# Linear attention into a gated long convolution on one core: another hand-written order of issue, and idle products at 14 places instead of 11

## The chip, the cores and the metric

The kernel runs on one core of a Trainium2 chip. Times are device microseconds, from the profile's clock or from timed runs of the whole program; the median of three timed runs is 264.11 us (264.1 to 265.25). Five engines work side by side, each through its own queue in order: TensorE (PE; its weight loads are PEld), VectorE (DVE), ScalarE (ACT), GpSimd (POOL) and SyncE (SP). In this kernel GpSimd and SyncE issue DMAs, and ScalarE issues one.

## What is computed

Two stages. The first is attention with random features, for 8 batches of 8 heads, 576 rows and 64 columns, with 128 features:

```python
h = proj - sq;  h = h - np.max(h, axis=-1, keepdims=True)
phi = np.exp(h) / np.sqrt(m)                   # proj = x @ omega.T, x = q or k, scaled
kv = einsum('bhsm,bhsd->bhmd', k_p, v);  z = sum(k_p, axis=2)
out = einsum('bhsm,bhmd->bhsd', q_p, kv) / (einsum('bhsm,bhm->bhs', q_p, z) + 1e-6)
```

The second takes that output as x (8 batches, 576 rows, 512 columns):

```python
x1, x2, x3 = split(x @ w_proj)
x2_conv = irfft(rfft(x2, axis=1) * rfft(filter, axis=0), n=576, axis=1)
y = (x1 * x2_conv * x3) @ w_out
```

## The kernel before, in words

**Tiling.** Each batch's 576 rows are four tiles of 128 and 64 rows left over; the left rows of two batches make one tile more ("left keys", "left queries", "left out"). Keys and queries are turned with TensorE (`transposes`) and copied to SBUF by VectorE or ScalarE. `key_features` and the query products go into PSUM, and ScalarE takes the exponential. `max_to_c` and `scale_values` weigh the values on VectorE (the factor that replaces the maximum). "Sums" is 40 products of 65 columns per batch, which ScalarE copies to `kv`. "Turn out" is eight products for each tile, `normalise` on VectorE, and a turn back (`turn_runs`, `turn_back`) into `xt`.

**Second stage.** "Gates" are the x1 and x3 products of `xt` with the weights, multiplied on VectorE. The transform over 576 points is products with small tables: 576 is 3 times 192, and the bins are kept in classes of even and odd ones. "Fold" and "rest" build the folded rows, "forward" transforms, SyncE moves halves of the spectrum to the other partitions (`sp`, `xw`), VectorE multiplies by the filter's spectrum, "inverse" transforms back, and "out" multiplies by w_out and stores.

**The filter.** `load_filter` loads the filter in two parts (288 KB each in SBUF), `fold_filter` folds them on VectorE, SyncE moves the pieces to `fd` and `fl`, `filter_transform` makes five groups of products, and `split_out` evicts each on ScalarE (two evictions) and sends it by SyncE to `hps` and `hqs`.

**What sets the order.** The program is not issued as it is written. The class `Plan` records every instruction (L182), numbers it (1,466 operations; products into one tile of one stage count as one), and `order` (L215) returns them in the order of the constant `ORDER` (L26), after it has made sure that data come before use. `issue` (L234) then issues them in that order; all recorded instructions carry line 250. Every engine's queue is therefore that list with the others' entries left out. Tiles that share a name share a few buffers, and these are handed out in the order of issue: the order also decides which batch's values share a buffer, and what a load has to wait for.

**Idle products.** `FILL` (L92) names operations on TensorE in front of which `issue` puts products of ones with ones (L239) into the bank that the operation is about to write; nobody reads them.

**Names used below.** Operations 1 and 6 load the two halves of batch 0's keys; 86 and 87 load the filter; 655 to 664 fold it on VectorE and 665 to 674 move the pieces on SyncE; 689, 682, 704, 697 and 675 are the filter's products. 110 scales batch 0's values, 119 is batch 0's sums, 120 their copy. 200 and 202 turn back batch 1's normalised rows. 220 loads batch 3's values, 349 the left values of batches 4 and 5.

Of the kernel before, what the change touches and what calls it, by code (L numbers as in the profile page):

```python
# [23 lines left out]
CROSSED = {"keys": 8, "queries": 8, "out": 8}  # L24

ORDER = """  # L26
25 34 39 32 38 40 35 37 33 36 31 28 29 30 4 42 49 41 43 50 51 6 0 1 3 56 55 21 139 5 22 44 68 45 24
10 75 137 46 62 23 64 63 9 2 54 52 53 57 65 83 60 59 58 76 61 81 7 66 82 78 89 141 90 14 613 48 69
209 91 101 103 85 70 47 84 142 92 80 93 138 102 612 94 95 96 72 74 67 11 77 157 79 71 611 73 112 114
158 104 615 160 116 151 12 105 106 107 152 145 162 118 627 159 115 161 154 117 221 153 156 155 111 8  # L30
20 16 87 108 109 97 99 110 119 19 210 113 98 120 167 614 168 163 164 127 128 121 122 183 165 184 129
130 123 131 18 132 15 124 125 126 148 86 174 176 185 166 186 133 177 227 630 169 170 222 140 187 134
178 180 179 100 228 171 172 233 135 229 136 173 175 231 616 655 657 628 629 147 146 149 619 17 658
716 647 656 234 649 181 672 235 182 673 212 247 211 236 248 194 621 625 660 144 195 674 639 668 188
196 189 620 190 245 641 246 191 640 197 192 193 626 198 199 319 320 224 648 226 642 623 722 650 202
215 13 203 281 204 200 201 205 206 143 689 691 690 675 676 659 696 622 663 724 679 255 695 219 150
618 617 792 692 223 216 214 213 624 661 677 237 238 634 225 794 694 257 731 662 793 207 788 643 715
208 645 795 239 230 259 261 664 666 681 717 293 240 720 671 725 669 294 287 288 232 732 790 651 295
249 723 719 670 297 693 321 665 323 322 737 290 292 218 733 789 250 241 251 635 721 252 734 738 296
298 260 217 678 283 667 791 253 243 254 644 680 357 262 256 258 780 646 242 289 358 711 718 282 263  # L40
299 782 291 697 264 268 269 712 276 351 345 220 277 270 278 631 636 300 653 698 301 682 302 713 699
714 265 266 273 267 274 684 363 704 309 706 244 364 311 705 683 781 735 736 726 275 303 729 783 304
305 306 702 366 359 688 739 707 652 700 368 686 361 740 637 638 313 365 785 784 315 367 420 360 362
654 307 308 346 369 747 314 728 370 727 786 385 386 787 317 316 751 318 748 271 272 310 340 755 341
342 429 312 430 752 753 749 750 756 327 335 387 388 754 328 730 336 279 757 381 329 796 337 280 764
893 348 284 382 687 371 758 332 423 285 372 632 333 334 417 957 959 685 798 710 797 424 389 343 344
373 892 765 324 432 325 799 383 969 894 899 374 709 326 708 421 492 766 896 352 703 745 434 384 741
396 746 971 398 88 286 760 759 898 762 338 339 742 961 958 633 425 884 701 761 431 427 970 960 743
963 354 433 744 330 331 962 763 972 375 897 376 392 964 395 901 355 803 903 377 907 908 895 817 885
390 482 888 349 353 394 379 347 819 902 378 889 769 814 805 770 985 815 800 987 802 801 816 977 916  # L50
917 979 804 806 905 807 808 818 820 821 809 399 823 886 906 397 810 822 499 455 400 887 456 426 391
914 824 393 915 825 500 826 900 773 774 428 978 912 811 812 771 412 772 767 913 768 909 413 414 439
776 775 980 827 501 910 986 493 409 481 911 494 440 904 410 503 856 857 865 866 932 858 933 930 931
988 411 495 497 415 862 416 863 419 356 928 973 975 929 778 777 779 974 976 441 842 844 401 402 403
350 845 843 847 864 867 934 487 831 833 935 937 404 846 828 830 829 442 418 405 849 851 406 965 967
813 435 437 832 848 496 502 936 918 834 850 436 443 852 836 483 438 919 890 835 859 853 891 504 966
944 860 945 938 837 855 968 838 924 925 553 498 554 922 839 939 940 923 407 408 449 450 981 452 451
1150 920 1152 446 380 457 840 1010 491 490 448 861 854 868 927 458 921 1012 983 444 453 454 869 559
1077 521 522 1085 517 1151 560 1153 996 459 445 505 1092 476 506 477 447 998 518 871 872 997 1000
1086 555 989 982 999 478 984 557 479 480 463 464 471 946 991 870 472 948 473 950 951 947 1087 873  # L60
465 926 942 460 461 523 877 841 878 1011 1013 1014 1088 1089 1090 507 519 1163 1162 524 520 941 488
1091 1078 949 1164 1158 1165 462 508 990 1107 952 468 879 992 466 469 470 1108 467 943 509 1093 510
1109 489 474 1160 525 953 475 1105 511 880 1007 1106 422 881 882 1009 1008 1079 1110 874 562 561 955
954 883 1080 993 1123 1159 564 994 1081 512 1124 995 532 875 1016 486 1101 956 1102 1094 1001 1002
1015 1161 534 1166 1024 1168 1096 1017 1003 526 1026 1154 1156 1038 513 1004 1098 1040 1127 1021 563
1022 1128 1006 1018 1005 1023 1155 1103 1104 531 556 558 533 1025 1125 484 485 1167 515 1019 1028
1157 1027 528 1126 530 1039 1121 1030 1082 1029 1031 1169 1032 1020 569 1122 876 535 527 536 529 585
586 1100 1170 1035 1036 1172 548 537 1095 1041 549 1083 1042 1115 1130 1129 1037 1044 538 550 539
565 1084 540 566 1116 567 568 1171 541 545 1043 542 1045 1034 1046 570 546 514 547 1099 543 544 1058
587 589 1117 1059 1118 1052 1053 1120 1054 1047 1097 551 552 1033 1119 1111 1112 588 1113 1114 1174  # L70
1064 580 575 1131 516 1347 1176 1065 577 1067 1132 1173 582 1133 1068 1203 571 1135 572 573 579 581
1205 1048 576 1349 578 1270 1271 574 1066 1069 1049 1175 1348 1177 1134 1350 583 1136 1143 1204 1206
1050 1051 1285 1278 1355 1139 584 1144 590 1190 1207 1140 1357 1137 606 1138 1189 1191 1061 591 592
607 1062 608 1063 1193 1279 1186 1182 601 602 1188 609 1187 593 603 1183 610 1280 1192 598 1141 1200
1184 594 1142 1351 1356 1282 1185 1201 1202 1209 1284 595 1302 1303 1353 599 600 1283 1208 1358 1281
1055 1352 1354 596 1145 1060 1146 1148 1056 597 1147 1300 604 605 1298 1299 1301 1057 1210 1149 1294
1073 1343 1195 1295 1287 1286 1074 1345 1076 1194 1075 1196 1197 1211 1213 1272 1217 1219 1273 1318
1231 1319 1316 1317 1233 1296 1297 1320 1214 1274 1275 1321 1232 1218 1215 1216 1199 1198 1070 1071
1212 1220 1235 1234 1221 1288 1072 1276 1277 1178 1228 1314 1180 1229 1315 1323 1322 1289 1222 1223
1224 1225 1230 1248 1344 1237 1236 1346 1310 1311 1249 1245 1179 1246 1247 1250 1312 1290 1292 1293  # L80
1363 1304 1181 26 1291 1365 1305 1313 1306 1359 1238 1361 1307 1308 1239 1241 1330 1309 1227 1266
1267 1324 1332 1325 1328 1326 1269 1268 1331 1333 1364 1382 1384 1327 1329 1366 1240 1383 1334 1385
1379 1335 1380 1386 1226 1387 1388 1251 1360 1252 1253 1381 1396 1398 1336 1397 1362 1389 1393 1260
1337 1395 1400 1399 1394 1242 1254 1261 1402 1390 1339 1401 1391 1403 1404 1405 1338 1341 1340 1342
1375 1367 1255 1243 1244 1369 1438 1439 1377 1262 1256 1441 1442 1435 1436 1443 1440 1437 1376 1410
1378 1392 1424 1411 1412 1407 1425 1426 1406 1408 1413 1414 1409 1428 1415 1371 1373 1421 1368 1263
1422 1423 1416 1427 1417 1372 1264 1429 1430 1418 1431 1265 1444 1445 1257 1370 1420 1432 1374 1434
1447 1446 1258 1259 1433 1419 1457 1451 1448 1458 1452 1463 1464 1449 1454 1450 27 1455 1460 1461
1462 1459 1453 1465 1456
"""  # L90

FILL = {  # L92
    22: (25,), 69: (3,), 72: (7,), 75: (17,), 78: (61,), 89: (4,), 91: (8,), 101: (4,), 103:
    (6,), 127: (6,), 157: (4,)
}

SIZE = {FP32: 4, UINT16: 2, BF16: 2, FP16: 2, mybir.dt.uint32: 4}


class Region:  # L100


    __slots__ = ("lo", "hi", "mask")

    def __init__(self, ap):
# [1296 lines left out]
```

## Time and profile before

| what | value |
|---|---|
| timed runs (median, range) | 264.11 us, 264.1 to 265.25 |
| the profiled execution, whole | 264.05 us |
| its span, first to last instruction | 262.3 us |
| mean granted TensorE clock | 0.993 |
| TensorE busy, products | 248.5 us, 95%, 2554 products (145 of them idle products) |
| VectorE, ScalarE, GpSimd busy | 230.8 us (88%), 212.9 us (81%), 59.6 us (23%) |
| last product ends, last store issued | 258.4 us, 259.0 us |

The page's second part cuts the span into 40 slices of 6.6 us; each digit is a busy share in tenths. The table of stretches gives, for a stretch in us: its length, then the busy time and the number of instructions of TensorE's products, its weight loads, VectorE, ScalarE and GpSimd, then the granted TensorE clock, the busy share of the DMA engines and the GB/s moved. A timeline row gives start, length, engine, line, operation, "out<-in", shapes and count; brackets hold the engine's idle time before it and what released it. In the chain that ended last, each row is start, length, and the work that held the end up at that time. Products are pipelined: a row's length holds the latency of its last product, so the next row can start before this one ends.

### The profile page before, as it was taken

What the parts mean: (1) busy time and instruction counts of PE and PEld (TensorE: products, weight loads), DVE (VectorE), ACT (ScalarE), POOL (GpSimd) and SP (SyncE); (2) the same over time, 40 slices, a digit from 0 to 9 for tenths busy, and PEclk for the clock granted to TensorE, in tenths of its full rate; (3) what the DMA queues carried; (4) which work ended last, traced back from release to release, by engine and by line L of the source; (5) the groups of instructions that cost most, each with busy time, mean ns of one, the idle gap of its engine ahead of it and who ended that gap; (6) DMA issues with size and microseconds to landing.
All of it is one profiled execution on the core that took longest, in us unless ns stands there. A gap on an engine that the chain in (4) does not pass through costs nothing.

```text
span 262.3 us, 6466 instructions
## 1 busy us (share of the span) xinstructions
PE 248.5 (95%) x2554; PEld 151.4 (58%) x2554; DVE 230.8 (88%) x549; ACT 212.9 (81%) x334; POOL 59.6 (23%) x80
## 2 busy tenths in 40 slices
PE   7977789999999999999999999999999999999994
PEld 6955656445547745645646655556457655456641
DVE  7899899998898997899989797999996889889980
ACT  5897498999999999869898779998996578567653
POOL 8393674440720093500314000000000000000000
PEclk9998899999999999999999999999999999999999
DMA  6999999999998599993692905103121421524626
GB/s 85 164 157 192 193 184 209 193 182 199 125 152 141 137 121 160 150 126 112 132 119 16 186 18 133 53 2 84 60 80 42 139 89 55 170 49 125 240 94 228
DMA packets 68854, 33.42 MB, mean 127 GB/s; under 512 B 39707, under 2 KB 63192, under 8 KB 68824
## 3 DMA queue, kind: packets, MB, share of 16 engines
q0 software_dynamic: 59088, 16.85, 63.2%
q1 hardware_dynamic: 9592, 15.96, 20.6%
q8 instruction: 20, 0.33, 0.5%
q10 hardware_dynamic: 144, 0.20, 0.2%
q14 instruction: 10, 0.08, 0.1%
HBM read 33.72 MB, written 9.44 MB: 165 GB/s over the span
## 4 chain that ended last, share of the span: by engine, by line
PE 60%; DMA 18%; DVE 10%; ACT 4%; POOL 3%; issue 2%; SPq 2%; DVEq 0%; POOLq 0%; ACTq 0%
PE h L250 48%; PE a L250 10%; DMA vl<-in_v_dram 4%; DMA vn<-in_v_dram 3%; DMA sp<-sp 3%; DVE sp L250 3%; DMA hps<-osb 3%; DMA sp<-x 2%; DMA kn<-in_k_dram 2%; PE a L239 2%; SPq L250 2%; DMA xw<-xr 1%; ACT osb L250 1%; DVE vc L250 1%; DVE xb L250 1%
## 5 line engine op out<-in xcount | busy, mean ns | idle before, releaser
L250 PE MATMUL h<-xt,wproj 128*128 128x512 bf16 x256 | 64.3, 379 | 0.1
L250 ACT CAST x<-h 128x512 bf16<-128x512 f32 x68 | 39.9, 600 | 9.0 <-PE h L250 8.3
L250 PEld LDWEIGHTS <-wproj 128*128 128x128 bf16 x384 | 30.8, 98 | 25.9 <-issue 2.4
L250 POOL DMA_DIRECT2D qn<-in_q_dram x26 | 23.2, 898 | 57.8 <-PE h L250 46.1
L250 ACT ACTIVATE eqt<-a 128x1024 bf16<-128x1024 f32 x32 | 33.0, 1048 | 3.0 <-PE a L250 2.8
L250 ACT ACTIVATE osb<-h 128x512 f32<-128x512 f32 (+4 forms) x53 | 29.6, 570 | 6.8 <-PE h L250 5.2
L250 ACT ACTIVATE ek<-a 128x1024 bf16<-128x1024 f32 x32 | 33.0, 1050 | 1.1 <-PE a L250 1.0
L250 PE MATMUL h<-wproj,xf 128*128 128x512 bf16 x128 | 32.1, 379 | 0.4 <-DVE kt L250 0.4
L250 PE MATMUL h<-wout,yt 128*128 128x512 bf16 (+2 forms) x132 | 31.4, 373 | 0.0
L250 DVE TENSOR_TENSOR x<-h,x 128x512 bf16<-128x512 f32 x32 | 21.9, 684 | 3.5 <-PE h L250 2.6
L250 DVE TENSOR_TENSOR xb<-a,rden 128x512 bf16<-128x512 f32 x36 | 24.2, 682 | 0.7
L250 ACT CAST sp<-h 128x512 bf16<-128x512 f32 x32 | 18.5, 596 | 4.8 <-PE h L250 4.8
L250 PEld LDWEIGHTS <-yt 128*128 128x128 bf16 x132 | 12.2, 98 | 13.0 <-DVE yt L250 0.4
L250 PEld LDWEIGHTS <-xf 128*128 128x128 bf16 x128 | 11.7, 98 | 13.1 <-issue 1.3
L250 PEld LDWEIGHTS <-sp 128*128 128x128 bf16 x160 | 13.7, 98 | 6.9 <-issue 1.0
L250 ACT COPY xt<-h 128x1024 bf16<-128x1024 bf16 x16 | 16.3, 1025 | 0.4 <-PE h L250 0.2
L250 PE MATMUL h<-x,fwb 128*128 128x512 bf16 x56 | 15.5, 379 | 0.0
L250 PE MATMUL a<-qt,om 64*128 64x512 bf16 x64 | 11.8, 383 | 2.0 <-ACT eqt L250 0.9
L250 PE MATMUL a<-om,kt 64*128 64x128 bf16 x256 | 11.8, 218 | 1.8 <-ACT ek L250 1.0
L250 ACT COPY qt<-h 128x1024 bf16<-128x1024 bf16 x12 | 12.1, 1016 | 1.7 <-PE h L250 1.7
L250 PEld LDWEIGHTS <-eqt 128*128 128x128 bf16 x256 | 11.1, 99 | 3.6 <-issue 0.7
L250 PE MATMUL a<-kv,eqt 128*128 128x65 bf16 x256 | 12.6, 195 | 0.4 <-DVE xb L250 0.4
(155 smaller groups left out, 532.7 us busy)
## 6 DMA issues: line engine op xcount, KB each, us to landing
out_dram<-osb SPq DMA_DIRECT2D x24, 256.0 KB, 2.2
vn<-in_v_dram POOLq DMA_DIRECT2D x8, 512.0 KB, 9.8
sp<-sp SPq DMA_DIRECT2D x16, 256.0 KB, 3.5
kn<-in_k_dram POOLq DMA_DIRECT2D x7, 512.0 KB, 9.7
qn<-in_q_dram POOLq DMA_DIRECT2D x24, 128.0 KB, 9.3
wproj<-in_moe_w_proj_dram POOLq DMA_DIRECT2D x3, 512.0 KB, 12.0
qn<-in_q_dram POOLq DMA_DIRECT2D x2, 512.0 KB, 8.9
out_dram<-xf SPq DMA_DIRECT2D x4, 256.0 KB, 2.0
```

The costliest lines, as they stand in the source:

```text
L239: self.nc.tensor.matmul(out=out[:, 0:cols], lhsT=self.ones[:, 0:P], rhs=self.ones[:, 0:cols], start=True, stop=True,)
L250: getattr(real, name)(*args, **kw)
```

## The change

Two constants are replaced, nothing else. `ORDER` is another permutation of the same 1,466 numbers, and `FILL` puts 167 idle products in front of 14 operations instead of 145 in front of 11. No instruction of the computation is added, removed or altered; the instructions stand otherwise on every engine's queue, nearly throughout.

```diff
 ORDER = """
-25 34 39 32 38 40 35 37 33 36 31 28 29 30 4 42 49 41 43 50 51 6 0 1 3 56 55 21 139 5 22 44 68 45 24
-10 75 137 46 62 23 64 63 9 2 54 52 53 57 65 83 60 59 58 76 61 81 7 66 82 78 89 141 90 14 613 48 69
-209 91 101 103 85 70 47 84 142 92 80 93 138 102 612 94 95 96 72 74 67 11 77 157 79 71 611 73 112 114
-158 104 615 160 116 151 12 105 106 107 152 145 162 118 627 159 115 161 154 117 221 153 156 155 111 8
+25 43 32 34 33 38 39 40 28 36 29 35 37 138 0 4 42 30 49 31 50 41 87 44 51 45 46 47 21 1 3 55 56 2 10
+86 9 5 22 54 67 52 142 53 143 139 24 62 63 64 57 58 6 59 7 60 23 61 81 65 83 66 82 69 70 71 72 655
+657 89 14 74 73 614 613 48 615 656 209 75 11 90 91 8 92 660 76 658 674 672 668 78 673 77 659 103 80
+93 94 95 611 96 101 104 116 79 105 115 117 118 102 144 106 19 97 151 616 107 152 108 112 111 114 113
+154 156 99 109 20 12 626 621 157 153 689 155 110 141 619 158 16 690 617 664 625 98 100 145 137 119
...
-1447 1446 1258 1259 1433 1419 1457 1451 1448 1458 1452 1463 1464 1449 1454 1450 27 1455 1460 1461
-1462 1459 1453 1465 1456
+1420 1440 1446 1264 1265 1435 1436 1437 1434 1433 1419 1447 1448 1449 1450 1460 1461 1462 1457 1458
+1454 1455 1459 1456 1463 1464 1465 1451 1452 1453
 """

 FILL = {
-    22: (25,), 69: (3,), 72: (7,), 75: (17,), 78: (61,), 89: (4,), 91: (8,), 101: (4,), 103:
-    (6,), 127: (6,), 157: (4,)
+    22: (26,), 69: (44,), 71: (48,), 72: (3,), 75: (3,), 89: (4,), 101: (6,), 103: (4,), 115:
+    (3,), 116: (8,), 119: (5,), 133: (3,), 151: (4,), 616: (6,)
 }
```

In the part shown: both filter loads (87, 86) now stand among the first four of GpSimd's loads, and the key half 1 in front of 6; the filter's folds (655 to 660) and four of its moves (674, 672, 668, 673) stand in the first attention stage; the filter product 689 stands right in front of the sums of batch 0 (119), where it stood behind the turn-back of batch 1 (202, 200). Of the part cut, these: SyncE's other six filter moves go forward with their folds; GpSimd's load of batch 6's values (422) stands in front of that of batch 3 (220), so batches 2, 3, 4, 5 and 7 share one values buffer where 3, 4, 5 and 6 did; and the load of the left values of batches 4 and 5 (349) stands before the loads of batch 5's queries, where it stood behind three of them. At the end the last product group is 1451 (512 columns, ScalarE, stored by SyncE), where it was 1460 (384 columns, stored by ScalarE).

## The prediction

> **What bounds the kernel now.** I read the page's busy rows and slices first, then the table of stretches, then the chain that ended last, then the timelines of TensorE and VectorE where that chain leaves TensorE.
>
> ```profile
> PE 248.5 (95%) x2554; PEld 151.4 (58%) x2554; DVE 230.8 (88%) x549; ACT 212.9 (81%) x334; POOL 59.6 (23%) x80
> ...
> PE   7977789999999999999999999999999999999994
> ...
> DVE  7899899998898997899989797999996889889980
> ```
>
> TensorE is short of full only in the first seven slices (to about 45 us) and in the last one. The change removes no arithmetic, so time can only come from that front, from single waits behind it, and from the tail. The next view is the table of stretches (busy time by engine, then granted clock).
>
> ```profile
> 0.00:23.97 23.97, 18.73 (x285) 15.59 (x285) 20.37 (x71) 18.99 (x24) 15.54 (x26) 1.00 1.26 145
> 23.97:44.82 20.85, 17.87 (x275) 13.62 (x275) 18.89 (x48) 14.66 (x20) 12.20 (x16) 0.92 1.59 194
> 20.90:24.30 3.40, 2.04 (x36) 1.57 (x37) 3.10 (x7) 3.40 (x5) 1.22 (x3) 1.00 1.58 190
> 24.30:27.70 3.40, 3.40 (x55) 3.40 (x52) 2.62 (x4) 1.13 (x2) 1.52 (x3) 0.50 1.60 189
> ```
>
> The third number group after the length is VectorE's: 39.26 us of work in the first 44.82, idle for 3.60 and then 1.96. VectorE sets the front; TensorE waits for its copies and evictions. At 44.82 VectorE ends batch 1's last normalised row, and at 45.21 TensorE turns those rows back. From there TensorE has a backlog. VectorE's timeline shows the one large hole of the second stretch:
>
> ```profile
> 25.59 0.68 DVE L250 TENSOR_TENSOR h<-h 128x1024 bf16<-128x1024 bf16 x1
> 27.06 0.69 DVE L250 COPY qt<-h 128x1024 bf16<-128x1024 bf16 x1 [0.79 <-PE h L250]
> 28.02 0.46 DVE L250 RECIPROCAL rden<-a 128x8 f32<-128x8 f32 x2 [0.27 <-PE a L250]
> ```
>
> It waits there (0.79 + 0.27) for TensorE, which works through the 40 products of batch 0's sums at clock 0.50. Behind 45 us, the chain and TensorE's own timeline name four waits that count:
>
> ```profile
> 59.47 6.21 DMA sp<-x
> ...
> 96.30 9.18 DMA vl<-in_v_dram
> ```
> ```profile
> 64.91 0.39 PE L250 MATMUL h<-sp,fwb 128*128 128x512 bf16 x1 [0.32 <-DMA sp<-x]
> 65.72 0.38 PE L250 MATMUL h<-sp,fwb 128*128 128x512 bf16 x1 [0.42 <-DMA sp<-x]
> ...
> 106.05 0.19 PE L250 MATMUL a<-vcl,ekl 128*128 128x65 bf16 x1 [0.20 <-DVE vcl L250]
> ...
> 112.16 1.02 PE L250 MATMUL h<-wproj,xf 128*128 128x512 bf16 x4 [0.35 <-DVE kt L250]
> ```
>
> Two are moves of the folded filter that land late (SyncE issued the last at 59.47). The third is the left values of batches 4 and 5, loaded at 96.30, and the fourth comes six microseconds behind it on ScalarE and VectorE, still late from it.
>
> **A yardstick.** Let TensorE's lag be the clock time at which a product starts, less the product work in front of it. Starts follow each other by 57 ns at 128 columns (61 idle products from 6.30 to 9.80), 215 ns at 512 (four from 40.74 to 41.60) and 31 ns at 65 (40 sums from 106.05 to 107.31); I use 55, 216 and 31. In front of 45.21 stand 237 real products of 128, 34 of 512 and 144 of 65 columns: 13.04 + 7.34 + 4.46 = 24.84 us. The lag is 20.37 us. It only grows by waits, and its end value sets the end.
>
> **The front, in the new order.** Instruction by instruction, the same turn-back of batch 1 now has 40.85 us of VectorE work in front of it: 1.45 of filter folding, 0.60 of zeroing, 0.49 of table copies and one gate product (0.69) come forward, 1.64 of table and sine work goes back (+1.59). TensorE has 25.27 in front of it (+0.43, two products of 512). With VectorE as idle as before (5.56) that start would be at 46.41 and the lag 21.14, so 0.77 worse. What speaks for less idle time: between the scaling of batch 0's values and the first normalisation that needs its sums, VectorE now has 3.0 us of independent work (zeros, table copies, a fold, one key copy). So the 1.06 hole should be covered. Up to the end of that scaling VectorE has 19.97 of work against 20.37 before, ended at 23.97. The scaling waited 0.17 for its load, which landed at 22.72. In the new order two filter loads (288 KB each) precede that load and a 512 KB and a 64 KB one now follow it: equal bytes, so about 22.7 again at latest, and 0.4 less at best. I take an idle 3.7 to there and 0.9 behind it: 40.85 + 4.6 = 45.45, lag 20.2, **a gain of 0.2**. Bounds: idle 3.9 in all gives 19.5 (gain 0.9), idle as before gives the loss of 0.77.
>
> **The idle products** rise from 145 to 167: 22 x 57 ns = 1.25 us of TensorE, nearly all ahead of the first keys. With one filter load ahead of it, the first half of batch 0's keys lands at about 5.80 + 1.5 = 7.3 (the second half followed the first by 1.39 per 256 KB); the 26 and 44 idle products end near 6.4. The 48 ahead of the first key products end near 10.6, and two key blocks are then through at 11.9, where ScalarE began its first exponential at 12.19. So they cost nothing; uncovered, the 48 would cost 2.7. The five in front of the sums cost 0.28 if VectorE is early.
>
> **The clock.** The Trainium skill, TensorE: Matmul & The Clock Gate, section Why this matters for your kernels, asks for no idle gap over some 3 us. This trace disagrees: the longest gap in 20.9 to 24.3 is 0.52 us, and the clock of the next stretch is 0.50. There TensorE was busy 2.04 of 3.40. By that rule neither kernel loses the clock; by the rows it goes with the busy share. In the new order that stretch holds three key blocks, a filter product, five idle products and the sums' start, some 2.6 us by the same starts against 2.2. I take a full clock. If it halves, the sums take 2.18 and not 1.26: 0.9, of which the 3.0 us of VectorE work lets 0.5 through.
>
> **The four waits behind it.** A wait costs its idle plus what pipelining hides (a 512-column row shows 0.38 but frees its successor after 0.216): 0.32 + 0.16, 0.42 + 0.17, 0.20 + 0.16 and 0.35 + 0.17, together 1.95 us. The left values of batches 4 and 5 can now be requested when 55 us of product work is done, not 70; they are needed at 85 in both, so that pair goes. The filter's folds move forward by about 10 us and so does SyncE's queue of moves; but the product that needs them comes forward too, from 44 to 31 us of product work (clock time 31.2 + 20.2 = 51.4). SyncE's last piece for it stands behind a fold that VectorE ends near 41.1 and six more issues (3.7 us by their rows): issued near 44.8, landing 6.2 later, at 51.0. That is a margin of 0.4 only. Batch 3's values now share a buffer with batch 2's: requested at 46 us of product work (about 67), landing within 4.0 (the queue empty, as the loads of 67.4 in the trace) to 11.4 (the queue full), needed at 77 by VectorE. GpSimd has stood idle for buffers by then, so I take the short end; the long one is 1.4 late. The q4, k6 and v4 loads queued behind them on GpSimd have over 20 us of product work in hand. I put 0.6 for new waits (bounds 0 and 1.6): **a gain of 1.35**.
>
> **The tail.** The last product group has 512 columns and not 384, so its eviction takes 0.60 and not 0.49; its store leaves from SyncE and not ScalarE, both issuing in about 0.35. **A loss of 0.1.**
>
> Sum: 0.2 + 1.35 - 0.1 = 1.45 us less. The profiled execution took 264.05 us (span 262.3), almost the median 264.11. Forecast: 264.05 - 1.45 = 262.6.
>
> **Rivals.** *No change:* VectorE keeps its 5.56 us of idle (+0.77), and the filter's wait comes back in full at its new place (1.1 of the 1.95): 264.05 + 0.77 - 1.95 + 1.1 + 0.1 = 264.1. For it speaks the 0.4 us margin; against it the work moved into the hole. *Slower, by one product:* the first filter product is moved from behind batch 1's turn-back to right in front of batch 0's sums on TensorE, with its two evictions in ScalarE's queue, one of them before the copy of the sums. It needs four SyncE moves. VectorE ends their folds near 14.6, four issues of 0.58 last to about 16.9, and at 5.6 each (the row of these moves) the last lands near 22.0, when TensorE arrives at 22.4. From a landing at 23.5 on, every microsecond goes through. The GpSimd loads of that stretch took 8 to 11 us; if the moves fared like those (10.3), they would land at 26.7, the sums start at 27.4, 3.2 past what VectorE's spare work hides: 265.8. Against it: at 39 to 46 us, with loads just as dense, the same moves took 5.6 while loads took 12. A measurement here can tell about 0.5%, so slower begins at 265.4, a landing near 26.3.
>
> **Chances.** Forecast 0.50, no change 0.32, slower 0.18; faster than 262.8 has the first, within 0.5% the second. Low end: front at its best (0.9), no new wait (1.95), tail: 264.05 - 2.75 = 261.3; I give 261.2. The high end takes in most of the slower case: 265.6.
>
> **What would show it.** Right: VectorE without a hole of 0.5 us or more from 24 to 45; batch 1's turn-back near 45.4; clock 1.00 throughout; no TensorE wait on the left values near 106. Wrong: TensorE idle in front of a filter product near 22 (the slower rival) or near 51 (no change); a half clock anywhere before 45; waits for value or query loads from 65 on.

## The result, and the profile after

The changed kernel takes 262.33 us (median of 16 runs, 260.85 to 266.06), the kernel before 264.51 us (16 runs on the same chip, 262.45 to 265.29): ratio 0.9924, 95% interval 0.9897 to 0.9952. Measured a second time, it gave 0.9943 (0.9912 to 0.9975). The forecast, 262.6 against 264.05, is a ratio of 0.9945. So the size was right. The profile says that terms behind it were not.

The profiled execution of the changed kernel took 264.32 us (span 262.5), 2 us over its median. Its times are therefore read for where it waits, not for the total. Busy rows and slices of its page:

```profile
PE 250.4 (95%) x2576; PEld 154.8 (59%) x2576; DVE 230.4 (88%) x549; ACT 211.5 (81%) x334; POOL 59.4 (23%) x80
...
PE   8985979999999999999999999999999999999993
...
DVE  6896799999888999998899999899998996989870
...
PEclk9997699999999999999999999999999999999999
```

The front fills seven slices here too, and two of them have a reduced clock. Its table of stretches:

```profile
0.00:23.62 23.62, 19.75 (x284) 16.87 (x284) 18.86 (x74) 17.63 (x22) 14.69 (x25) 1.00 1.24 152
23.62:30.44 6.82, 5.77 (x75) 4.85 (x75) 4.66 (x12) 3.12 (x5) 4.27 (x5) 0.50 1.53 194
30.44:37.50 7.06, 5.09 (x77) 3.60 (x75) 6.92 (x15) 5.39 (x8) 3.00 (x4) 1.00 1.78 183
```

The clock is at half for 6.82 us, where the kernel before had 3.40. VectorE (third group) works 18.86 of the first 23.62 us. What holds the engines is in the timelines, TensorE's first and then VectorE's:

```profile
24.53 0.59 PE L250 MATMUL h<-sp,fwa 128*128 128x512 bf16 x1 [1.96 <-DMA sp<-yt]
...
37.49 0.39 PE L250 MATMUL a<-qt,om 64*128 64x512 bf16 x2 [1.43 <-ACT eqt L250]
...
104.47 0.24 PE L250 MATMUL h<-gta,sp 128*128 128x192 bf16 x1 [0.52 <-DVE x L250]
...
106.96 0.19 PE L250 MATMUL a<-vcl,ekl 128*128 128x65 bf16 x1
...
254.80 1.47 PE L250 MATMUL h<-wout,yt 128*128 128x384 bf16 x7 [0.30 <-DVE yt L250]
```
```profile
24.31 1.23 DVE L250 TENSOR_TENSOR vc<-vn,vc 128x2048 bf16<-128x2048 bf16 x1 [2.13 <-DMA vn<-in_v_dram]
...
29.83 0.21 DVE L250 RECIPROCAL rden<-a 128x8 f32<-128x8 f32 x1 [1.21 <-PE a L250]
```

The filter product 689 stands 1.96 us for its last move. The chain gives that move as

```profile
16.49 7.91 DMA sp<-yt
24.53 1.01 PE h L250 x2
```

so it was issued at 16.49 as forecast (16.9) and took 7.91 us, not the 5.6 that I took from the row of before. Batch 0's values landed near 24.3, not 22.7. This is the mechanism of my slower rival, in part. Batch 1's turn-back starts at 47.64; the lag there is 22.4 us against 20.4 before. In this execution the front is 2.0 us worse.

Behind the front, everything that the sum counted on is there: no wait in front of the sums of batch 4 (106.96, no bracket), none for the filter's moves near 51 to 66, none at the gates near 112. TensorE's time beyond its nominal starts, from 45 us to the end, is +0.96 us before and -1.0 us after (nominal starts are slightly generous): 1.96 us gained there. Two waits are new, at 104.47 and at 254.80. The last product starts at 258.05 where it started at 258.08. In the two profiled executions front and rest cancel; in the median they do not.

### The profile page after: what moved, and what is told of

It reads as the page before. It is cut to its first block, busy times and chain, and to the rows that moved or that the text cites. A ratio compares the mean times of both kernels' runs of the same rounds, so it can differ in the third digit from the quotient of the medians.

```text
span 262.5 us, 6509 instructions
## 1 busy us (share of the span) xinstructions
PE 250.4 (95%) x2576; PEld 154.8 (59%) x2576; DVE 230.4 (88%) x549; ACT 211.5 (81%) x334; POOL 59.4 (23%) x80
## 3 DMA queue, kind: packets, MB, share of 16 engines
q1 hardware_dynamic: 9592, 15.96, 20.7%
## 4 chain that ended last, share of the span: by engine, by line
PE 73%; ACT 8%; DVE 7%; DMA 7%; issue 2%; SPq 1%; ACTq 0%; DVEq 0%
PE h L250 58%; PE a L250 11%; DMA sp<-yt 3%; PE h L239 3%; DMA hqs<-osb 3%; ACT ek L250 2%; ACT osb L250 2%; DMA out_dram<-osb 2%; SPq L250 1%; PE a L239 1%; ACT x L250 1%; DVE xb L250 1%; ACT qt L250 1%; DVE yt L250 1%; DVE vc L250 1%
## 5 line engine op out<-in xcount | busy, mean ns | idle before, releaser
L250 PE MATMUL h<-xt,wproj 128*128 128x512 bf16 x256 | 64.2, 379 | 0.0
L250 PEld LDWEIGHTS <-wproj 128*128 128x128 bf16 x384 | 30.8, 98 | 25.8 <-issue 1.6
L250 ACT CAST x<-h 128x512 bf16<-128x512 f32 x68 | 39.9, 606 | 7.5 <-PE h L250 6.0
L250 ACT ACTIVATE osb<-h 128x512 f32<-128x512 f32 (+4 forms) x53 | 30.3, 576 | 6.6 <-PE h L250 6.2
L250 ACT ACTIVATE eqt<-a 128x1024 bf16<-128x1024 f32 x32 | 32.3, 1037 | 3.3 <-PE a L250 3.1
L250 ACT ACTIVATE ek<-a 128x1024 bf16<-128x1024 f32 x32 | 32.8, 1040 | 2.5 <-PE a L250 2.2
L250 PE MATMUL h<-wproj,xf 128*128 128x512 bf16 x128 | 32.3, 379 | 0.0
L250 PE MATMUL h<-wout,yt 128*128 128x512 bf16 (+2 forms) x132 | 31.4, 373 | 0.3 <-DVE yt L250 0.3
L250 POOL DMA_DIRECT2D qn<-in_q_dram x26 | 23.2, 901 | 29.3 <-PE h L250 27.1
L250 DVE TENSOR_TENSOR x<-h,x 128x512 bf16<-128x512 f32 x32 | 21.9, 683 | 3.8 <-PE h L250 3.7
L250 DVE TENSOR_TENSOR xb<-a,rden 128x512 bf16<-128x512 f32 x36 | 24.5, 685 | 0.4
L250 ACT CAST sp<-h 128x512 bf16<-128x512 f32 x32 | 18.9, 596 | 1.8 <-PE h L250 1.1
L250 PEld LDWEIGHTS <-yt 128*128 128x128 bf16 x132 | 11.9, 98 | 12.9 <-DVE yt L250 0.8
L250 PEld LDWEIGHTS <-xf 128*128 128x128 bf16 x128 | 11.6, 98 | 12.3 <-issue 0.8
L250 PEld LDWEIGHTS <-sp 128*128 128x128 bf16 x160 | 13.8, 98 | 5.8 <-DVE bt L250 1.0
L250 ACT COPY xt<-h 128x1024 bf16<-128x1024 bf16 x16 | 16.2, 1026 | 0.2
L250 PE MATMUL h<-x,fwb 128*128 128x512 bf16 x56 | 15.7, 379 | 0.0
L250 PEld LDWEIGHTS <-eqt 128*128 128x128 bf16 x256 | 12.0, 100 | 4.9 <-DVE xb L250 0.5
L250 PE MATMUL a<-kv,eqt 128*128 128x65 bf16 x256 | 13.6, 197 | 0.5 <-DVE xb L250 0.3
L250 PE MATMUL a<-om,kt 64*128 64x128 bf16 x256 | 12.4, 220 | 1.7 <-DVE kt L250 0.7
L239 PEld LDWEIGHTS <-hps 128*128 128x128 bf16 x167 | 12.2, 114 | 2.6 <-issue 1.1
L250 PE MATMUL a<-qt,om 64*128 64x512 bf16 x64 | 11.9, 384 | 1.9 <-ACT eqt L250 1.6
```

The source lines that it names most:

```text
L239: self.nc.tensor.matmul(out=out[:, 0:cols], lhsT=self.ones[:, 0:P], rhs=self.ones[:, 0:cols], start=True, stop=True,)
L250: getattr(real, name)(*args, **kw)
```

## The experiments

Each row is compared with the kernel before on the same chip; "before" is its median there.

| run | median us | before | ratio, 95% interval |
|---|---|---|---|
| old_front_new_rest | 272.94 | 264.17 | 1.0334 (1.0287 to 1.0382) |
| new_front_old_rest | 264.82 | 264.17 | 1.0039 (1.0005 to 1.0074) |
| filter_product_later | 263.90 | 264.17 | 0.9998 (0.9965 to 1.0031) |
| changed_again | 263.02 | 264.17 | 0.9943 (0.9912 to 0.9975) |
| values_first | 263.36 | 264.06 | 0.9974 (0.9947 to 1.0002) |
| values_first_filter_later | 264.78 | 264.06 | 1.0003 (0.9969 to 1.0036) |
| old_idle_products | 266.95 | 264.06 | 1.0111 (1.0064 to 1.0159) |
| left_values_late | 261.99 | 264.06 | 0.9910 (0.9871 to 0.9950) |
| no_idle_before_keys | 261.27 | 263.63 | 0.9903 (0.9866 to 0.9939) |
| no_late_idle | 260.58 | 263.63 | 0.9875 (0.9831 to 0.9920) |
| gate_first_old_tail | 262.62 | 263.63 | 0.9938 (0.9905 to 0.9971) |
| no_idle_at_all | 260.26 | 264.96 | 0.9839 (0.9804 to 0.9875) |

### Front and rest exchanged

old_front_new_rest takes the order of before up to the turn-back of batch 1 (its first 258 entries), with its idle products, and then the changed order for what is left; new_front_old_rest does the reverse (259 entries). The seam is the place where the two orders meet.

```diff
-ORDER of the changed kernel, FILL of the changed kernel
+ORDER, old_front_new_rest: that of before up to "204 200", then the changed one without these; FILL of before
+ORDER, new_front_old_rest: the changed one up to "201 202", then that of before without these
```

> The order of before up to the turn-back of batch 1 (with its idle products), and the order of the change for all that follows. My theory, that the gain lies in the waits behind the front: ratio to before 0.993 (about 262.6 us), the TensorE waits on the left values near 106 us and on the late key copy near 112 us gone, the filter's wait near 65 us gone or under 0.4. Rival, that the gain lies in the front and the rest gives back what it takes: ratio 0.999 to 1.001.

> The order of the change up to the turn-back of batch 1 (with its idle products), and the order of before for all that follows. My theory: the front gives 0.2 us and the early folds take the filter's wait away (1.1), while the left values' two waits (0.9) stay: ratio 0.995 to 0.997. Rival, that the whole gain lies in the front: ratio 0.992. A third, that the front loses what its profile shows (2.0 us of TensorE's lag, from the first value load and the filter's four moves): ratio 1.002 to 1.006.

Both came out slower than the kernel before, the first by 3.3% where I had expected a gain of 0.7%, the second by 0.4%. TensorE's timeline of the first:

```profile
52.76 0.40 PE L250 MATMUL a<-om,kt 64*128 64x128 bf16 x8 [1.49 <-DVE xb L250]
57.79 0.59 PE L250 MATMUL h<-sp,fwb 128*128 128x512 bf16 x2 [2.00 <-DMA sp<-x]
62.08 0.58 PE L250 MATMUL h<-sp,fwb 128*128 128x512 bf16 x1 [3.70 <-DMA sp<-x]
```

In the order of before only five of the ten folds and four of the ten moves stand ahead of the seam. The new rest asks for the filter at once and stands 5.70 us for it; the 1.49 us ahead of that and a half clock from 59.02 to 65.85 come on top. So the early folds and moves do not shorten the front; they are what the front pays so that the rest need not wait. Neither half of the change is a gain alone. new_front_old_rest has four waits at its seam (0.46, 0.63, 0.55, 0.22 us), one of 0.50 us at 212.22, and the gates' wait near 112 again (0.21), so its 1.0039 says only that the new front brings no gain that outweighs a seam of about 1.9 us. The gates wait there although the sums of batch 4 no longer do (106.92, no idle time in front of them): the fourth wait of the forecast is not, or not only, an after-effect of the third.

### The two late transfers of the front

Three kernels take the two transfers off the front's path, one by one and together. A fourth is the changed kernel unaltered.

```diff
 ORDER, filter_product_later
-621 157 153 689 155 110 141 ... 167 168 227 174 228 ... 620 15 176 175 221 ... 158 16 690 617
+621 157 153 155 110 141 ... 167 168 227 689 174 228 ... 620 15 176 690 691 175 221 ... 158 16 617
 ORDER, values_first
-657 89 14 74 73 614 613 48 615 656 209 75 11 90 91 8 92
+657 89 14 8 74 73 614 613 48 615 656 209 75 11 90 91 92
```

> The changed kernel with one product (the first filter product) and its two evictions moved back, from right in front of batch 0's sums to behind the first key turn of batch 2; all else as it is. If the four moves alone held the sums up (TensorE stood 1.96 us in front of it in the profile): 1.5 to 2 us below the changed kernel, ratio to before 0.985. If batch 0's values land as late as the moves do (VectorE stood 2.13 us for them in the same profile, ending at 25.53 where TensorE was free at 25.87): at most 0.4 us below it, ratio 0.991.

> The changed kernel unaltered, for a second profile of its front beside the others of this call. If the late landings of the first profile (values 24.3 us, filter moves 24.4 us, half clock for 6.8 us) are its ordinary state: the same again, with a span near 262.5. If they are one draw of several: values nearer 22.7, TensorE's stand in front of the filter product under 1 us, and a span 1.5 to 2 us shorter. Ratio to before 0.9924 either way.

> The changed kernel with one load moved: batch 0's values (operation 8) are issued by GpSimd in front of the left keys' load (209) that waits for a buffer, so at about 8.2 us and not at 14.2. My theory: in the changed kernel batch 0's values land at 24.3 and hold VectorE for 2.1 us, but the filter product 689 in front of the sums is held to 24.5 by its own moves, so each of the two alone takes away little. Expected: the scaling starts at 22.5 or earlier without a wait for its load; TensorE still stands in front of 689 for over 1 us; batch 1's turn-back near 47 instead of 47.6 to 48.0; ratio to the kernel before 0.991 (0.988 to 0.995). Rival: the values' load was the whole of it; then the turn-back comes near 45.5 and the ratio is 0.985 or less. Second rival: the load only trades places with batch 1's left keys and the first exponentials, and the front loses elsewhere: ratio 0.998 or more.

> Both: batch 0's values issued at about 8.2 us, and the filter product 689 (with its two evictions) behind the queries' products of batch 1 instead of in front of batch 0's sums. If the front is held by these two transfers (my theory), no wait of 0.5 us or more is left on TensorE or VectorE from 21 to 30, the clock stays at 1.00, the turn-back of batch 1 starts near 45.5 to 46, and the time is near 260.3: ratio to before 0.985 (0.982 to 0.989), a version faster than the changed kernel. Rival: the front then waits for ScalarE (exponentials and copies, as the 1.43 us in front of the queries' turn-out at 37.5 in the changed kernel), and the turn-back stays at 47 or later: ratio 0.992 or more, no better than the changed kernel.

The unaltered kernel shows the late landing again (scaling at 24.91, the filter product at 24.71, turn-back at 47.09). But no repair gained anything. With the product moved back, TensorE waits at other places, in its timeline of filter_product_later:

```profile
24.20 0.29 PE L250 MATMUL a<-vc,ek 128*128 128x65 bf16 x4 [0.78 <-DVE vc L250]
...
34.93 0.39 PE L250 MATMUL a<-qt,om 64*128 64x512 bf16 x2 [0.93 <-ACT eqt L250]
38.07 0.39 PE L250 MATMUL a<-klt,om 64*128 64x512 bf16 x2 [0.63 <-ACT eqt L250]
38.98 0.19 PE L250 MATMUL a<-vcl,ekl 128*128 128x65 bf16 x1 [0.52 <-ACT ek L250]
```

ScalarE's exponentials take over: 2.08 us in three waits, where the changed kernel has 1.43 in one. (This execution, 262.31 us, was faster than the kernel's median of 263.90; what made the median no better is not in it.) With the values issued first, VectorE waits for the load that now lands behind them (VectorE's timeline of values_first):

```profile
22.63 0.42 DVE L250 TENSOR_TENSOR vcl<-vl,vcl 64x512 bf16<-64x512 bf16 x1 [1.49 <-DMA vl<-in_v_dram]
```

and the scaling of the values follows only at 23.63. GpSimd issues these loads one behind the other, and here the earlier place of one was a later landing of another. With both edits the query products slip instead (111 at 22.67, where it stood at 20.15 to 20.5), and half a clock window falls at 15.9. My theory that the two transfers alone hold the front falls. The turn-back of batch 1 comes at 46.13, 46.29 and 47.60 in the three, inside the 45.10 to 47.64 of the front as it was: behind the late transfers stand other waits, on ScalarE and on the other loads, that are about as long.

### The left values of batches 4 and 5

```diff
 ORDER, left_values_late
-... 391 349 899 ... 432 355 425 ...
+... 391 899 ... 432 355 354 353 88 419 349 425 ...
```

> The changed kernel with one load moved back: the left values of batches 4 and 5 (349) are issued by GpSimd behind the loads of batch 5's queries, the weights and batch 6's first queries, so at about 96 us, as in the kernel before, and not at 82.0. My theory: the two waits that the change removed come back: TensorE stands for the scaled left values in front of the sums of batch 4 near 106 to 107 (0.2 to 0.8 us) and is late at the gates near 112 (0.3 us or more); about 0.9 us in all, ratio to before 0.9975 (0.995 to 1.000). Rival: the wait was hidden by TensorE's backlog or moved to the next wait anyway, and the ratio is the changed kernel's, 0.994 or less, with no TensorE wait over 0.2 us at either place.

No wait came back, and the ratio is the changed kernel's. GpSimd issued the load at 94.47, VectorE used it without a wait (timelines of GpSimd and VectorE):

```profile
94.47 0.73 POOL L250 DMA_DIRECT2D vl<-in_v_dram  x1
```
```profile
105.16 0.41 DVE L250 TENSOR_TENSOR vcl<-vl,vcl 64x512 bf16<-64x512 bf16 x1
```

It landed 7.3 us later, at 101.8. Before, the same load left at 96.30 and took 9.18, to 105.48. So it came 3.7 us earlier, 1.8 of them by its issue and 1.9 by its flight. The load's new place at 82.0 removes the wait with some 16 us to spare, but the rest of the new order removes it without that place too. The kernel also gives a sample of the changed front with no late landing: filter product at 22.90, clock 1.00, turn-back at 45.10 (lag 19.8). It then stands 1.04 us in front of the filter product 682 at 52.27, and 1.25 in front of inverse 0 at 103.56 where the changed kernel stands 0.52 and 0.75 in its two profiles. What an early front gains, the rest gives partly back.

### The new waits

gate_first_old_tail moves VectorE's scaling of batch 4's values and two small steps behind the two gate products in front of inverse 0, and takes the order of before from about 236 us on.

```diff
 ORDER, gate_first_old_tail
-377 390 434 817 395 789 819 917 797 902 889 791 799 397
+377 434 817 395 789 819 917 797 791 799 390 902 889 397
 and from entry 1373 on the order of before
```

> The changed kernel mended at its two new waits. VectorE's scaling of batch 4's values and two rest and fold steps (390, 902, 889) go behind the two gate products that free the PSUM bank of inverse 0 (791, 799), and from 236 us on the order is that of the kernel before. Expected by the theory that the new waits are 800 in front of inverse 0 (0.7 to 0.9 us) and the tail's 1460 with the wait of ScalarE for a store's buffer (0.5 us): no TensorE wait over 0.3 us at 103 to 105 and at 253 to 255, sums of batch 4 still without wait, ratio to before 0.990 (0.986 to 0.994), 0.5 to 1.2 us less than the changed kernel. Rival: VectorE is the one that is late there, so the wait only moves to the sums of batch 4 or to the last outputs, and the ratio is the changed kernel's, 0.993 to 0.995.

```profile
104.51 0.26 PE L250 MATMUL h<-gta,sp 128*128 128x192 bf16 x1 [0.46 <-DVE bt L250]
```

The tail's wait is gone, the other only changes its name: 0.52 for the gate product becomes 0.46 for VectorE's next step. The ratio, 0.9938, is the changed kernel's: the rival's number.

VectorE is late there, and its timeline in the changed kernel says for what:

```profile
100.83 0.43 DVE L250 TENSOR_TENSOR xw<-xw,hqs 128x512 bf16<-128x512 bf16 x1 [0.39 <-DMA hqs<-osb]
```

It waits for the last piece of the filter's spectrum, which SyncE sends. From there to the gate product for which inverse 0 waits it has no other such wait. In the six profiles that keep the changed order at this place and show the wait, VectorE stands 0.39, 0.39, 0.62, 0.78, 1.13 and 1.14 us for this piece, and TensorE then 0.52, 0.52, 0.75, 0.91, 1.25 and 1.27 in front of inverse 0: always 0.12 or 0.13 more. In gate_first_old_tail VectorE stands 0.72 for it. So the edit moved steps that were not the cause; a kernel that sends this piece earlier was not tried.

### The idle products

Four kernels have the changed order with other idle products.

```diff
-FILL of the changed kernel (167)
+old_idle_products: FILL of before (145)
+no_idle_before_keys: the changed one without 69: (44,) and 71: (48,) (75 left)
+no_late_idle: only 22: (26,), 69: (44,), 71: (48,), 72: (3,), 75: (3,) (124 left)
+no_idle_at_all: FILL = {}
```

> The changed order with the idle products of the kernel before (145 at its 11 places instead of 167 at 14). My theory: the idle products are covered by the first loads and evictions and do not hold the clock: the same time as the changed kernel, ratio to before 0.994 (0.991 to 0.997), with a half clock near 24 to 30 as in the changed kernel. Rival: they hold the clock up, and without them the granted clock falls below the changed kernel's in the first 24 us: ratio 0.998 or more. Other rival: the 22 more cost their 1.25 us, ratio 0.990 or less.

> The changed kernel without the 44 and the 48 idle products in front of the turns of batch 0's first keys and of the first key products (75 of its 167 are left, 26 of them at the very start). With the earlier kernel's idle products the changed order was 1.1% slower than the kernel before, and its 128-column products took about 115 ns each until 16.0 us, where the changed kernel's take 57 ns from about 6.5 us. Theory now: idle products in that place bring the clock to full before the first keys. Expected: TensorE idle for over 2 us before the first keys, products at about 115 ns until 13 us or later, batch 1's turn-back at 48.5 or later, ratio to the kernel before 1.000 to 1.012. Rival: the earlier run lost its time because the old places put 61 and 17 idle products into busy stretches of the new order; then this kernel is as fast as the changed one, ratio 0.994 or less.

> The changed kernel without its idle products at the nine later places (43 of 167; the 124 ahead of the first keys stay). Theory: those 43 lie in waits and the clock there is decided by the real work: ratio to before 0.9945 (0.991 to 0.998), full clock from about 6.5 us as in the changed kernel, half clock for 0 to 7 us somewhere between 20 and 31 as in the changed kernel's own executions. Rival: they hold the clock; then half clock appears already between 10 and 20 us, and the ratio is 1.000 or more.

> The changed order without any idle product (0 of 167). The run without the 43 later ones was 0.7% faster than the changed kernel and showed the query products and the exponentials behind them 0.7 us earlier; the run without the 92 ahead of the first keys showed 128-column products at about 115 ns until 13 us, and lost nothing. Theory: both hold together, because TensorE waits for loads and VectorE there: query products near 17 us, ratio to the kernel before 0.988 (0.984 to 0.992), as good as without the 43 alone. Rival: without any of them the clock stays low through the query products and batch 0's sums (products of 115 ns until 20 us or later), and the gain is gone: ratio 0.994 or more.

In old_idle_products 61 idle products now stand in a busy place (TensorE's timeline):

```profile
16.75 3.58 PE L239 MATMUL a<-hps 128*128 128x128 bf16 x61
20.26 0.62 PE L250 MATMUL a<-om,kt 64*128 64x128 bf16 x16
```

They are named by operation, so an order and its idle products belong together. This kernel also runs at half clock until 16.0 us, but no_idle_before_keys does so until 13.3 and is not slower for it, so the place is the likelier cause. After that run I believed that the change's idle products earn their time by bringing up the clock. The next three refute it: none of them is slower than the changed kernel, and without any idle product it is clearly faster. With none, 260.26 us and 0.9839 (0.9804 to 0.9875) lie clear of the changed kernel's 0.9897 to 0.9952: some 0.9%, 2.2 to 2.7 us by its two ratios. It beats both kernels. (The two were not timed on one chip; the medians as they stand, 260.26 against 262.33 and 263.02, differ by 2.1 and 2.8 us.)

For the 43 later ones the trace shows a part of how. ScalarE's first query exponential in the changed kernel, and then without the 43 (where L249 is the line that was L250):

```profile
18.30 1.02 ACT L250 ACTIVATE eqt<-a 128x1024 bf16<-128x1024 f32 x1 [1.58 <-PE a L250]
```
```profile
17.41 1.94 ACT L249 ACTIVATE eqt<-a 128x1024 bf16<-128x1024 f32 x2 [0.84 <-PE a L249]
```

In front of it, TensorE's queue holds 21 idle products (at 103, 101, 116 and 115), 1.2 us at 57 ns, between the key products and the query products. ScalarE stands idle for TensorE there, 1.58 us; without them 0.84. The exponential starts 0.9 us sooner (0.76 to 1.05 against the four executions with the same front that I compared), and the turn-back of batch 1 comes at 44.62, the earliest with the changed order. The loads were early in this execution too (the values' scaling starts at 22.46), so the 0.9 us isn't shown to reach the turn-back. The ratio 0.9875 (0.9831 to 0.9920) overlaps the changed kernel's a little.

Why the 92 ahead of the first keys are no help either is told less well. Without any, TensorE runs slowly for long (its timeline, no_idle_at_all):

```profile
16.16 1.89 PE L248 MATMUL h<-ident,qn 128*128 128x128 bf16 x16
17.98 1.04 PE L248 MATMUL a<-qt,om 64*128 64x512 bf16 x4
```

From 16.16 to 17.98 it starts 16 products, 114 ns each, twice the 57 of a full clock, and the first record of a full clock is at 21.2 us. It costs next to nothing: the query products start at 17.98 where they started at 17.27 with all idle products. That profile is of the kernel's slowest run (261.84; the other five 259.86 to 260.80), so it doesn't show what the fast ones gained. What the three profiles share lies behind the front, where no idle product stands. From the turn-back of batch 1 to the start of the last product TensorE takes 210.41 and 210.04 us in the changed kernel, and 209.20, 208.82 and 208.81 without the 92, the 43 and all. Both new waits, at inverse 0 and at the last outputs, are missing: VectorE finds the piece of the spectrum landed (no_late_idle):

```profile
97.04 0.42 DVE L249 TENSOR_TENSOR xw<-xw,hqs 128x512 bf16<-128x512 bf16 x1
```

SyncE issues the last two pieces in 1.23 or 1.24 us there, in 1.77 and 2.22 in the changed kernel. Why it does is not shown; filter_product_later, with all 167, has 1.72 and no wait either.

What stays open, besides, is why no idle product at all is better than no late ones, if it is (the intervals overlap), and whether the later stretches at half clock are rarer for it: no_idle_at_all shows none from 21.2 us to its last product, and the mean clock of its six runs is 0.996 to 1.000, where the changed kernel's runs go down to 0.984.

## Why the prediction was right in its size, point by point

In short: the mechanism, four waits behind the front that go away, was right. That the sum came so near was in part luck, since errors in several terms offset each other.

**The waits behind the front: right, one cause overstated.** Forecast a gain of 1.95, less 0.6 for new waits. All four waits are gone in the profile after. The exchange of front and rest shows that the filter's waits depend on the early folds (5.70 us without them). For the left values, the step "can now be requested when 55 us of product work is done, not 70 ... so that pair goes" is not what decides: requested at 94.47, the pair was gone all the same. There the load left 1.8 us earlier than before and took 1.9 us less; which part of the new order does that is not shown.

**The new waits: wrong in place, and about twice the size.** Forecast 0.6, at the filter product near 51 or at batch 3's values. In the changed kernel's own two profiles neither waits; inverse 0 loses 0.69 and 0.91 us beyond its nominal start, and the last outputs 0.47 and 0.40, so 1.16 and 1.31 in all, within the bound of 1.6. The step that failed is the list of what could be late: it had the filter's fold moves and the loads, and not the last piece of the spectrum. Small waits that I hadn't counted went away as well, some 1.2 and 1.8 us, and the net gain behind 45 us is 1.96 us in the first profile and 2.4 in the second, against the forecast's 1.35. Only where the front was early did the filter product stand, 1.04 us: the margin of 0.4 that I gave it is real, and a late front hides it.

**The front: not shown.** Forecast a gain of 0.2 (bounds -0.77 to +0.9). The failed step is "about 22.7 again at latest" for batch 0's values: they landed at 24.3, and "at 5.6 each (the row of these moves) the last lands near 22.0" gave 24.4. The row was from 39 to 41 us. In the front the same move took 7.9. VectorE's work up to the last normalised row was 39.95 us and not 40.85, its idle time 7.53 and not 4.6; in left_values_late, where the loads came early, 40.21 and 4.73. So the work was put 0.6 to 0.9 us too high, and the idle time is what varies. Five executions of the changed front (two of the changed kernel, and those of new_front_old_rest, left_values_late and gate_first_old_tail) have a lag at batch 1's turn-back of 22.4, 21.8, 20.7, 19.8 and 20.4 us; the order of before has 20.4, and 21.5 in old_front_new_rest. Means of 21.0 and 20.9: no gain and no loss, with a scatter of 1 us that one profile cannot see through. My front term was an argument about tenths in a stretch that varies by microseconds.

**The hole of 1.06 us.** It was to be covered by 3.0 us of VectorE's spare work. It is 1.21 in the profiled execution, where the sums came 1.9 us later and all 40 ran at half clock (25.87 to 28.2), and absent in changed_again, left_values_late and filter_product_later. The cover works up to its size.

**The clock: wrong.** I took a full clock; three of those five executions have one or two half-clock windows of 3.4 us. The rule of the Trainium skill (TensorE: Matmul & The Clock Gate, Why this matters for your kernels: no idle gap over some 3 us) is not what is seen: the half clock begins at 23.6, about 1 us into a gap of 1.96, and the gap of 1.43 us in front of 37.49 leaves the clock full. That the clock goes with the busy share, as I read it, was the better reading. In the 3.41 us ahead of the half clock TensorE was busy for 1.71 us here, 1.62 in changed_again and 2.04 in the kernel before; stretches of the same length with 2.21 (33.85 to 37.26) and 2.29 (17.48 to 20.89 of before) were followed by a full clock. The share alone doesn't settle it: 1.98 us in changed_again, from 34.19 on, left the clock full. I put 2.6 us there and so took the wrong branch; the late moves made it 1.71.

**The idle products: wrong.** "So they cost nothing" covered only those ahead of the first keys. The 43 others I did not place one by one; 21 of them stand on the path from TensorE to ScalarE, and removing all 167 is worth as much as the whole change or more (0.9839 against 0.9924 and 0.9943). The order of before carries such products too, so that the error may cancel between the two kernels; that the sum came out right in spite of it is luck as far as the runs show. Whether the kernel before would gain as much without its own was not tried.

**The tail: right in sign.** Forecast a loss of 0.1. From the last `yt` (254.74 after, 254.72 before) to the last store's issue it is 4.69 against 4.67 us. The loss lies in front of it, the 0.47 us for which TensorE waits for `yt`.

**Slower, by one product.** Its mechanism occurred in both profiles of the changed kernel: the last move landed at 24.4, past the 23.5 from which it was to decide, so 0.9 us by its own rule and not the 3.2 of its price. Net it cost nothing that a run showed: with the product moved away the ratio is 0.9998, no better.

## What to carry to other kernels

Where loads and several engines limit a stage almost alike, moving one transfer or one product only names the next limit; when an engine is late, follow it back to what it waited for before moving its work, as at inverse 0; look for the gain where an engine has a backlog and stands for one late item, as here behind the front. Test filler work by leaving it out, all of it: here the kernel without any was the fastest. Before arguing over tenths of a microsecond in a stage that starts from loads, see how much the stage varies between executions of the same order.

## What the runs showed of the hardware

- The landing of the same load in the same order varied by 2.5 us between executions: batch 0's values let the scaling start at 22.44 to 24.91 us.
- The mean granted clock goes with the time. Of 28 runs of the changed kernel, the 15 with a clock of at least 0.996 have a median of 261.85 us, the 13 others 263.43. For the kernel before it is 263.52 (24 runs) and 264.59 (58 runs). A late transfer makes TensorE idle and so may lower the clock, or the lower clock may make the rest late; which of the two it is was not told apart.
- The row of clocks shows 9 from the first slice on, but 128-column products start every 111 to 114 ns in the first microseconds, and the first record of a full clock comes at 4.2 to 6.9 us with the changed order's idle products ahead of the keys, at 13.3 without those 92, at 21.2 without any. So these kernels start at half clock, and the row doesn't show it.
